# A new order of all steps, and of the products of zeros between them, in a fused local-attention and feed-forward kernel

## The chip, the core and the metric

The kernel runs on one core of a Trainium2 chip. A core has a matrix engine (TensorE, PE in the rows; its loads of stationary operands are PEld), a vector engine (DVE), a scalar engine with function tables (ACT), a general engine (GpSimd, POOL) and an engine that here issues all transfers (SyncE, SP). Each runs its own list of instructions in order; an instruction that needs another engine's result waits on a semaphore, and all that stands behind it on its engine waits too. The metric is the device time of one execution in microseconds.

## What is computed

```python
scores = scale * np.matmul(q, k.transpose(0, 1, 3, 2))        # q, k, v: 8 x 8 heads x 576 x 64
mask_plain = (rel >= 0) & (rel < 32)                          # heads 0 to 3
mask_dil = (rel >= 0) & (rel < 128) & (rel % 4 == 0)          # heads 4 to 7
scores = np.where(masks, scores, -1e9); scores -= max
attn = np.exp(scores); attn = attn / (sum + 1e-9)
x = (attn @ v) -> 4608 tokens x 512
h = x @ w_in                                                  # 512 x 2048
sp = np.where(h > 20.0, h, np.log1p(np.exp(np.minimum(h, 20.0))))
out = (h * np.tanh(sp)) @ w_out                               # mish, then 2048 x 512
```

The weights arrive as 64-bit floats. Products run in 16-bit floats with each operand split into a high and a low part, three products for one.

## The kernel before

The work is cut into sixteen units (a batch and half of its 576 rows each, 288 tokens). For one unit the steps are: loads of q and k (`ld`) and of v (`lv`), scales and splits of these (`pr`), scores of a pair of heads on PE (`sp`), the row maximum on DVE (`sc`), exponentials on ACT (`ex`), a transpose of the probabilities (`tp`: on PE for the first four units, by a transposing DMA for the others), the product with v and the division (`va`: PE, ACT, DVE), the transpose of the result (`tx`), then the feed-forward part: scales (`fs`), sixteen first products with mish on ACT (`ff`), the split of a quarter of the hidden layer (`gt`: ACT and DVE, for five quarters ACT and GpSimd), and sixteen second products of twelve matmuls (`fo`), the last of each four followed by scaling and a store.

The weights are prepared beside the first units, in pieces: load (`wl`), a pass of ACT over the upper words (`wm`), the rebuilding of 32-bit words on DVE (`ww`, lines 397 to 401), a sum over partitions on PE with a scale from it on DVE (`ws`, lines 367 to 388), and the split into high and low halves (`wp`, lines 412 to 426: ACT and DVE, for some pieces also GpSimd). `w.0.3.1` style numbers mean layer, column block, half.

Nothing plans at run time: a table of names, `ORDER`, fixes the order of all steps of all engines. A step is a generator; each time its name comes up it issues its next part, so that `va1.4` stands three times: products, denominators, division. The instructions of each engine run in the order in which they are issued:

```python
for name in ORDER:
    if name not in begun:
        ...
        if name[:2] == "kw":
            fn(int(name[2:]))
            continue
        begun[name] = fn(...)
    if hasattr(begun[name], "__next__"):
        next(begun[name], None)
```

`kwN` issues N products of a 128 x 128 block of zeros (line 922) into the last of four PSUM banks that `ff` and `fo` take in turn. They compute nothing that is used; they fill time in which PE's next real work isn't ready. `fs` (lines 831 to 833) makes small scales on DVE. Lines 759 and 761 are the reciprocal and the division of `va`, lines 717, 787 and 790 transposes on PE, line 804 the lower half of a transposed result.

Of the kernel before, what the change touches and what calls it, by code (L numbers as in the profile page):

```python
# [42 lines left out]
va0.1 sp0.1 tp0.7 va0.1 kw2 va0.7 ld1 sc0.2 wp0.0.1 sc0.3 va0.7 va0.1 ex0.2 pr1 kw16 kw16 kw7 tp0.4 ex0.3 kw5 tp0.2
kw13 tx0.0 wm0.1.0 va0.7 wp0.0.0 kw10 tx0.3 tp0.4 tp0.2 ww0.1.0 tx0.0 wl0.2.1 kw16 kw1 va0.2 tx0.3 ww0.1.0 tx0.0 tx0.0
kw11 tx0.3 va0.4 va0.2 va0.4 kw2 tp0.5 tx0.3 va0.2 tp0.5 va0.4 kw16 tp0.3 va0.5 wp0.0.1 sp1.0 va0.5 tp0.3 va0.5
wm0.2.0 wl0.1.1 sc1.0 kw8 sp1.1 sc1.1 ex1.0 sc1.2 kw14 va0.3 wm0.2.1 tx0.2 lv2 sc1.3 kw2 pr1 va0.3 tx0.2 va0.3 ex1.3
pr1 kw16 kw6 tx0.2 ww0.2.0 tp1.0 ld2 tx0.2 tx0.1 pr1 ww0.2.1 tx0.1 fs0.0 ex1.2 pr1 kw16 kw1 tx0.1 ws0.2 tx0.1 tp1.0
ww0.2.1 ff0.12 ex1.1 wm0.1.1 ff0.13 ff0.12 ww0.1.1 ws0.2 va1.0 tp1.2 ff0.13 tp1.1 ff0.14 ww0.2.0 va1.0 wp0.2.1 ws0.1
ff0.14 tp1.1 ff0.15 va1.0 tp1.2 wp0.2.0 ws0.1 va1.2 ww0.1.1 ff0.15 ff0.0 va1.2 wp0.1.0 sp1.2 ff0.0 gt0.3 tp1.3 sc1.4
ff0.3 wp0.1.1 va1.2 ff0.2 sc1.5 tp1.3 ff0.3 wp0.2.0 sp1.3 ff0.2 ex1.4 wp0.2.1 va1.1 wl1.3.0 va1.3 ff0.1 sc1.7 va1.1  # L50
va1.3 ex1.5 sc1.6 ff0.8 ex1.7 va1.3 va1.1 ex1.6 tp1.4 ff0.9 fs0.2 ff0.1 wp0.1.1 tx1.0 tx1.1 wp0.1.0 ff0.8 ff0.11 tx1.0
tp1.4 gt0.3 wl1.3.1 gt0.0 tp1.5 tx1.0 va1.4 wl1.1.0 ff0.10 fs1 tp1.5 gt0.0 tx1.1 wl1.1.1 ff0.9 tx1.1 ff0.4 tx1.0 pr2
wm1.3.0 va1.5 va1.4 tp1.6 ff0.11 tp1.7 tp1.6 fs0.1 ff0.7 va1.5 va1.4 ff0.10 tp1.7 va1.5 ff0.4 va1.6 va1.7 va1.6
wm1.3.1 tx1.2 va1.6 lv3 ff0.6 va1.7 tx1.2 va1.7 gt0.2 ww1.3.1 kw7 tx1.3 tx1.2 sp2.0 ww1.3.0 tx1.3 gt0.0 ff0.5 sc2.1
tx1.2 ff0.7 tx1.3 ws1.3 ff0.6 gt0.2 tx1.3 ff0.5 sc2.0 ff1.8 ex2.1 ws1.3 pr2 ff1.4 pr2 ex2.0 ww1.3.0 ff1.5 wm1.1.0
tp2.0 ff1.8 sp2.1 ww1.1.0 ww1.1.0 pr2 ff1.11 ld3 ff1.4 wm1.1.1 ff1.10 tp2.0 ww1.1.1 ff1.5 pr2 ff1.9 ff1.11 gt0.1 sc2.2
ff1.6 sc2.3 wp1.3.0 gt0.1 ws1.1 ff1.10 wp1.3.0 ff1.9 ex2.2 ff1.0 ww1.3.1 wl1.2.1 ff1.7 ex2.3 ws1.1 va2.0 ff1.6 tp2.2
tp2.1 fo0.3.0 ww1.1.1 tp2.2 va2.0 va2.2 wp1.3.1 ff1.2 ff1.0 wp1.3.1 fo0.3.1 tp2.1 wp1.1.0 wp1.1.1 wl1.2.0 fo0.3.2
va2.0 wp1.1.1 pr3 fo0.3.3 va2.2 wm1.2.1 va2.1 wp1.1.0 ff1.7 sp2.3 va2.2 fo0.3.3 ff1.3 wp1.1.1 sc2.6 ww1.2.1 wl1.0.0
va2.1 gt1.2 fo0.1.0 sc2.7 wp1.1.1 va2.1 wm1.2.0 fo0.1.1 gt1.2 wl1.0.1 ff1.2 sp3.2 ff1.3 fo0.3.3 ww1.2.0 ex2.7 gt1.2  # L60
ff1.1 sc3.4 ex2.6 fo0.1.2 ww1.2.1 gt1.1 sp3.1 ex3.4 fo0.1.3 sc3.2 gt1.1 ff1.1 ff1.12 sc3.5 gt1.1 sc3.3 tp2.3 ff1.12
ws1.2 tp2.3 ww1.2.0 gt1.0 va2.3 ws1.2 wm1.0.0 ff1.13 va2.3 sp3.0 va2.3 fo0.1.3 tp2.7 sc3.0 tx2.0 tp2.7 ff1.14 wm1.0.1
gt1.0 tx2.0 ff1.15 wp1.2.1 tx2.0 sc3.1 tp2.6 fo1.1.0 ff1.13 ww1.0.0 ff1.15 ww1.0.1 ex3.0 sp2.2 ws1.0 sc2.4 ld4 ex3.1
sc2.5 ex2.4 wp1.2.1 fo1.3.0 tp2.6 ex2.5 wp1.2.0 tx2.1 fo1.1.1 ww1.0.0 ff1.14 ws1.0 wp1.2.0 va2.6 fo1.3.1 tx2.1 va2.6
wp1.0.0 va2.7 wp1.2.0 tx2.1 tp2.4 fo1.3.2 va2.6 tx2.1 wp1.2.0 va2.7 tp2.4 va2.7 fo1.1.2 gt1.3 pr4 ex3.5 tx2.3 gt1.3
pr3 va2.4 fo1.2.0 gt1.3 tx2.3 fo1.2.1 va2.4 tx2.3 wp1.0.0 pr3 tp2.5 pr3 tp3.0 tp2.5 pr3 fo1.1.3 tp3.0 va2.4 wp1.0.0
ww1.0.1 va2.5 fo0.2.0 ex3.2 wp1.0.0 tp3.1 fo1.3.3 tp3.1 va2.5 va2.5 va3.0 pr4 tx2.2 fo1.2.2 tx2.2 fo1.1.3 fo1.1.3
# [911 lines left out]
```

## Time and profile before

| | us |
|---|---|
| median of 3 runs (lowest to highest) | 930.99 (930.51 to 931.06) |
| profiled execution | 931.03 |
| its span | 929.2 |
| PE busy | 918.5 (99%) |
| DVE busy | 647.5 (70%) |
| ACT busy | 565.7 (61%) |
| GpSimd busy | 57.3 (6%) |
| products of zeros, busy | 42.0, 646 of them |

A busy share is an average over the whole span: it counts products of zeros like others, and in the first 60 us PE's busy time is mostly these. Matmuls overlap in the pipeline, so a row's time for some matmuls in a row is longer by the tail of the last than the distance to the next row's start. Rows in order of time give the start, the duration, the engine, the line, the instruction with its tiles, how many, and in brackets how long the engine sat idle before and for whom. Waits are listed by who waited for whom.

### The profile page before, as it was taken

Reading aid. Unit: us, or ns where it says so; the run is one execution under the profiler, and the core shown is the slowest. Engines: PE = TensorE matmul, PEld = TensorE weight load, DVE = VectorE, ACT = ScalarE, POOL = GpSimd, SP = SyncE. Lnnn points to the kernel's source line nnn. Section 1 sums busy time; section 2 is a strip of 40 time slices with the busy share of each in tenths; the row PEclk is TensorE's granted clock in tenths of the full one; section 3 lists DMA queues with packets and bytes.
Section 4 is the critical chain, followed back from the end, with each engine's and each line's share of the span. In section 5 each row is a group of like instructions: output and inputs, shape, how many; then the busy total and the mean of one; then the engine's idle time right before and its main releaser. Section 6 shows DMA issues by size and latency. Waiting matters only on the chain.

```text
span 929.2 us, 22966 instructions
## 1 busy us (share of the span) xinstructions
PE 918.5 (99%) x9558; PEld 745.0 (80%) x9562; DVE 647.5 (70%) x1352; ACT 565.7 (61%) x1086; POOL 57.3 (6%) x116
## 2 busy tenths in 40 slices
PE   9999999999999989999999999999999999999998
PEld 9988877888778778788878888877888787888876
DVE  4998987558585697997687887877686786524120
ACT  2888977566666547577566665747576563745241
POOL 1001064401000000000000000000000000000000
PEclk9999999999999999999999999999999999999999
DMA  7656341121413225262517232535315322121100
GB/s 258 196 167 209 114 143 52 59 74 42 96 40 98 76 70 131 58 146 43 141 29 155 60 112 45 119 89 93 89 40 100 79 55 61 28 68 41 47 1 26
DMA packets 158104, 82.44 MB, mean 89 GB/s; under 512 B 124496, under 2 KB 153904, under 8 KB 158000
## 3 DMA queue, kind: packets, MB, share of 16 engines
q1 hardware_dynamic: 158000, 80.97, 35.0%
q8 instruction: 75, 1.23, 0.5%
q14 instruction: 29, 0.24, 0.1%
...
## 4 chain that ended last, share of the span: by engine, by line
PE 92%; DVE 5%; ACT 1%; issue 1%; DMA 0%; SPq 0%; DVEq 0%; ACTq 0%
PE f L894 39%; PE f L843 38%; PE psc L617 4%; PE f L922 3%; PE pav L744 3%; PE pav L738 1%; PE ptp L717 1%; DVE raw L399 1%; DVE nm L648 1%; DVE m L309 1%; DVE raw L401 0%; PE psc L614 0%; ACT hm L848 0%; DVE raw L412 0%; PE pm L367 0%
## 5 line engine op out<-in xcount | busy, mean ns | idle before, releaser
L843 PE MATMUL f<-x,w 128*128 128x288 f16 x3072 | 393.3, 286 | 1.7 <-ACT hm L848 1.7
L894 PE MATMUL f<-g,w 128*128 128x288 f16 x3072 | 393.2, 287 | 0.0
L894 PEld LDWEIGHTS <-w 128*128 128x128 f16 x3072 | 296.7, 98 | 74.9
L843 PEld LDWEIGHTS <-w 128*128 128x128 f16 x3072 | 295.5, 98 | 76.0 <-issue 2.2
L848 ACT ACTIVATE hm<-f,fs 128x288 f32<-128x288 f32 x256 | 119.6, 497 | 103.5 <-PE f L843 96.8
L884 DVE SCALAR_TENSOR_TENSOR g<-hm,sg,g 128x1152 f16<-128x1152 f32 x59 | 82.9, 1409 | 40.5 <-ACT g L882 40.5
L906 ACT ACTIVATE y<-f,fo 128x288 f32<-128x288 f32 x60 | 41.8, 718 | 99.6 <-PE f L894 74.2
L882 ACT ACTIVATE g<-hm,sg 128x1152 f16<-128x1152 f32 x59 | 73.9, 1253 | 0.6
L759 DVE RECIPROCAL rec<-den 96x3 f32<-96x3 f32 (+1 forms) x128 | 21.3, 167 | 68.1 <-ACT den L755 56.5
L650 DVE TENSOR_TENSOR sb<-sb,nm 96x256 f32<-96x256 f32 (+3 forms) x120 | 56.4, 470 | 4.1
L761 DVE TENSOR_TENSOR xs<-pav,rec 96x192 f32<-96x192 f32 (+1 forms) x128 | 49.6, 387 | 11.2 <-DVE rec L759 0.9
L648 DVE TENSOR_REDUCE nm<-sb 96x2 f32<-96x256 f32 (+3 forms) x120 | 53.7, 448 | 3.3
L670 ACT ACTIVATE sb<-sb,ln_p 96x352 f32<-96x352 f32 (+3 forms) x96 | 53.5, 586 | 0.2
L755 ACT ACTIVATE den<-pav 96x3 f32<-96x3 f32 (+1 forms) x96 | 14.7, 162 | 62.8 <-PE pav L744 62.5
...
L642 DVE SCALAR_TENSOR_TENSOR sb<-psc,sc,m_r 96x352 f32<-96x352 f32 (+1 forms) x48 | 28.4, 592 | 24.3 <-PE psc L617 24.1
L922 PE MATMUL f<-zeros 128*128 128x128 f16 x646 | 42.0, 224 | 1.1 <-DVE zeros L918 1.1
...
L922 PEld LDWEIGHTS <-zeros 128*128 128x128 f16 x646 | 39.1, 101 | 1.9 <-DVE zeros L918 1.0
L776 ACT CAST g<-xs 96x384 f16<-96x384 f32 (+1 forms) x48 | 26.8, 562 | 19.9 <-DVE xs L761 17.6
L642 DVE SCALAR_TENSOR_TENSOR sb<-psc,sc,m_s 72x288 f32<-72x288 f32 (+1 forms) x48 | 27.6, 574 | 11.3 <-PE psc L617 11.2
...
## 6 DMA issues: line engine op xcount, KB each, us to landing
...
```

Source lines behind the costliest of these rows:

```text
L642: nc.vector.scalar_tensor_tensor(shaped(sb), shaped(pt), d["sc"][:nq], mask, ALU.mult, ALU.add)
L648: nc.vector.tensor_reduce(nm[:nq, j:j + n], x, axis=AX.X, op=ALU.max, negate=True)
L650: nc.vector.tensor_tensor(o, x, nm[:nq, j:j + n].unsqueeze(2).broadcast_to([nq, n, w]), op=ALU.add)
L670: nc.scalar.activation(x, x, AF.Exp, bias=ln_p[:nq])
L761: nc.vector.tensor_tensor(xs[:nq, :nb, (head % 2) * D:(head % 2 + 1) * D], avv[:, :, :D], rc.unsqueeze(2).broadcast_to([nq, nb, D]), op=AL ...
L843: nc.tensor.matmul(ph[:, :HT], w1[j][:, c, wi, k * P:(k + 1) * P], x_of(d, xi, c), start=(n == 0), stop=(n == len(seq) - 1))
L848: nc.scalar.activation(d["m"][j][:, k], ph[:, :HT], AF.Mish, scale=d["fs"][:, j:j + 1])
L882: nc.scalar.activation(g[:, 0], m, AF.Identity, scale=sg)
L884: nc.vector.scalar_tensor_tensor(g[:, 1], m, sg, g[:, 0], ALU.mult, ALU.subtract)
L894: nc.tensor.matmul(po[:, :HT], w2[:, e, j, wi, k * P:(k + 1) * P], d["g"][j][:, gi, k, :], start=(j == 0 and n == 0), stop=(j == NCH - 1 a ...
L906: nc.scalar.activation(o, src, AF.Identity, scale=fo)
L922: nc.tensor.matmul(fbs[3][:, 512 - P:], zeros, zeros, start=True, stop=True)
```

## The change

Only the table `ORDER` is another one. Each step stands in it as often as before; the `kw` entries alone differ in number: 54 entries with 646 products before, 52 with 598 now. Before, 639 of the products stand before the first `ff` step and 7 behind the fifteenth; now 553 stand before the first, and 28, 2, 6 and 9 behind the eighth, ninth, eleventh and twelfth. The table's first line, before and after:

```diff
 ORDER = """
-lv0 wl0.3.0 wl0.3.1 ld0 wl0.0.0 wl0.0.1 pr0 kw16 kw16 kw16 kw16 kw16 kw16 kw16 kw16 kw3 pr0 pr0 kw10 pr0 wm0.3.0
+wl0.3.1 wl0.3.0 ld0 lv0 wl0.0.1 wl0.0.0 wm0.3.1 ww0.3.1 ww0.3.1 wm0.3.0 ww0.3.0 ww0.3.0 kw16 kw16 kw16 kw16 kw16 kw16
```

What it moves is seen in the engines' lists. The transfer queue SP at its start, before: values of unit 0 (`vn`, `vdn`), then the first two pieces of weights (`raw`), then q and k.

```order
L473 DMA vn<-in_v 128x4x64 x3
L475 DMA vdn<-in_vd 72x4x64 x4
L341 DMA raw<-in_w_in 128x512 x4
L447 DMA qn<-in_qT 128x1152
L449 DMA knp<-in_kT 128x2x288
L452 DMA knd<-in_kdT 128x4x72 x2
L341 DMA raw<-in_w_in 128x512 x6
```

SP at its start now:

```order
L341 DMA raw<-in_w_in 128x512 x4
L447 DMA qn<-in_qT 128x1152
L449 DMA knp<-in_kT 128x2x288
L452 DMA knd<-in_kdT 128x4x72 x2
L473 DMA vn<-in_v 128x4x64 x3
L475 DMA vdn<-in_vd 72x4x64 x4
L341 DMA raw<-in_w_in 128x512 x8
```

The four weight transfers moved from behind the seven of the values to the head, and the values behind q and k. DVE follows: the two reductions over unit 0's values (line 309) stood first there, and stand now behind the first weights' split (line 418).

The second place is DVE near the end of unit 2's attention. Before, `ws` is the scale chain of a piece of the second layer (its last two rows here), line 412 two passes over raw weights, lines 759 and 761 the two divisions that fill `xs`, which PE transposes next; line 804 is the lower half of that transpose.

```order
L387 RECIPROCAL r_o_2599<-f_o_105 128x1
L388 TENSOR_SCALAR ws4_2593<-f_1_104,r_o_2599 128x4
L412 TENSOR_SCALAR raw_2207<-raw_2207,ws4_2593 128x512 x2
L759 RECIPROCAL rec_2651<-den_2622 72x4
L761 TENSOR_TENSOR xs_2608<-pav_2603,rec_2651 72x4x64
L759 RECIPROCAL rec_2659<-den_2656 72x4
L761 TENSOR_TENSOR xs_2608<-pav_2626,rec_2659 72x4x64
L309 TENSOR_REDUCE m_2677<-qn_2536 128x1
L804 TENSOR_TENSOR x_2440<-px_2681,x_2440 128x4x72
```

The same two divisions and what follows them now:

```order
L759 RECIPROCAL rec_2561<-den_2555 72x4
L761 TENSOR_TENSOR xs_2525<-pav_2520,rec_2561 72x4x64
L397 TENSOR_SCALAR w2_103<-w2_103 128x1024
L759 RECIPROCAL rec_2586<-den_2582 72x4
L761 TENSOR_TENSOR xs_2525<-pav_2564,rec_2586 72x4x64
L399 SCALAR_TENSOR_TENSOR raw_2177<-raw_2177,w2_103 128x1024
L397 TENSOR_SCALAR w2_103<-w2_103 128x1024
L399 SCALAR_TENSOR_TENSOR raw_2340<-raw_2340,w2_103 128x1024
L804 TENSOR_TENSOR x_2445<-px_2611,x_2445 128x4x72
L418 SCALAR_TENSOR_TENSOR w2_103<-raw_1948,ws4_2310,w2_103 128x512 x2
L374 TENSOR_REDUCE wm4_2671<-pm_2627 128x4
```

The scale chain (it begins with line 374) and the raw passes moved behind the transpose's lower half, and work on weight words (lines 397, 399) stands among the divisions.

The third place is DVE and PE in unit 1's attention, where unit 0's first `ff` products are under way. DVE now:

```order
L418 SCALAR_TENSOR_TENSOR w_100<-raw,ws_1435,w_100 128x2x512
L831 TENSOR_SCALAR fs<-f_104,f 128x1
L832 RECIPROCAL sg<-fs 128x1
L833 TENSOR_SCALAR sg<-sg 128x1
L759 RECIPROCAL rec<-den 72x4
L761 TENSOR_TENSOR xs<-pav,rec 72x4x64
```

In the old list one scale step of unit 1, on four columns at once, stood near this place, behind a gate; now two steps of unit 0 do, on one column each, ahead of and behind a division. PE now, down to the first of nine zeros, behind which the next transpose (`ptp`) waits for the division above:

```order
L843 MATMUL f_111<-x,w_101 128x288
L717 MATMUL ptp<-ident,sb 104x72 x4
L790 MATMUL px<-ident,xs 128x96 x3
L738 MATMUL pav<-vdn,pp 72x65 x4
L922 LDWEIGHTS zeros
L922 MATMUL f_111<-zeros 128x128
```

PE before, at the same transposes of unit 1, with no zeros among them:

```order
L843 MATMUL f_108<-x,w_100 128x288
L738 MATMUL pav<-vdn,pp 72x65 x4
L717 MATMUL ptp<-ident,sb 104x72 x8
L843 LDWEIGHTS w_100
L843 MATMUL f_109<-x,w_100 128x288
```

The last two transposes of the unit's probabilities stood together between `ff` products; now one stands ahead of the nine zeros and one behind.

## Rows read from the trace of the kernel before

**Rows 1.** The page's first part: busy time, share and instructions of each engine.

```profile
PE 918.5 (99%) x9558; PEld 745.0 (80%) x9562; DVE 647.5 (70%) x1352; ACT 565.7 (61%) x1086; POOL 57.3 (6%) x116
```

**Rows 2.** PE's waits: line, for whom; us in total, times, longest.

```profile
PE px L790 <- DVE xs L761: 1.9, 1, 1.9
PE f L843 <- ACT hm L848: 1.7, 2, 1.2
PE pav L744 <- DMA pT<-p: 1.6, 1, 1.6
PE f L922 <- DVE zeros L918: 1.1, 1, 1.1
PE px L787 <- ACT pp L726: 0.3, 1, 0.3
PE ptp L717 <- DVE rec L759: 0.2, 1, 0.2
```

**Rows 3.** PE in order of time: start, the first ff products, the end.

```profile
1.05 9.35 PE L922 MATMUL f<-zeros 128*128 128x128 f16 x131 [1.05 <-DVE zeros L918]
...
11.30 7.71 PE L922 MATMUL f<-zeros 128*128 128x128 f16 x135
18.85 1.06 PE L367 MATMUL pm<-w,ones 128*128 128x512 bf16 x3
...
58.34 3.10 PE L843 MATMUL f<-x,w 128*128 128x288 f16 x24
...
901.83 23.68 PE L894 MATMUL f<-g,w 128*128 128x288 f16 x192
```

**Rows 4.** Stretches: length, busy PE, PEld, DVE, ACT, POOL, granted clock, DMA, GB/s.

```profile
21.50:55.10 33.60, 33.09 (x510) 30.08 (x509) 31.07 (x73) 25.57 (x66) 0.24 (x2) 1.00 0.68 210
155.00:165.00 10.00, 8.13 (x61) 5.99 (x59) 4.97 (x15) 3.98 (x7) 5.99 (x5) 0.83 0.01 2
340.00:900.00 560.00, 560.00 (x5762) 449.56 (x5761) 385.63 (x799) 334.57 (x642) 8.18 (x53) 1.00 0.35 76
```

**Rows 5.** The transfer queue SP in order of time, at the start.

```profile
6.31 2.02 SPq L341 DMA_DIRECT2D raw<-in_w_in  x4
```

**Rows 6.** ACT in order of time, the first passes over weights.

```profile
13.53 1.16 ACT L356 ACTIVATE w<-raw 128x1024 f32<-128x1024 f32 x1 [2.70 <-DMA raw<-in_w_in]
16.06 1.17 ACT L356 ACTIVATE w<-raw 128x1024 f32<-128x1024 f32 x1 [1.37 <-DMA raw<-in_w_in]
```

**Rows 7.** DVE in order of time, at the start.

```profile
5.42 0.95 DVE L309 TENSOR_REDUCE m<-vn 128x1 f32<-128x768 f32 x1 [4.42 <-DMA vn<-in_v]
8.13 1.22 DVE L309 TENSOR_REDUCE m<-vdn 72x1 f32<-72x1024 f32 x1 [1.76 <-DMA vdn<-in_vd]
...
22.64 0.16 DVE L379 RECIPROCAL ws<-f 128x1 f32<-128x1 f32 x1
```

**Rows 8.** PE in order of time, around its longest wait.

```profile
152.51 3.11 PE L894 MATMUL f<-g,w 128*128 128x288 f16 x24
157.49 0.44 PE L790 MATMUL px<-ident,xs 72*128 72x72 f32 x4 [1.87 <-DVE xs L761]
...
158.40 4.78 PE L894 MATMUL f<-g,w 128*128 128x288 f16 x24
```

**Rows 9.** DVE in order of time, ahead of that wait.

```profile
150.72 1.15 DVE L375 TENSOR_SCALAR wf<-wm 128x4 int32<-128x4 int32 x1
...
152.96 2.81 DVE L412 TENSOR_SCALAR raw<-raw,ws 128x512 int32<-128x512 int32 x2
```

**Rows 10.** GpSimd in order of time, the same stretch.

```profile
149.03 2.81 POOL L422 TENSOR_TENSOR raw<-raw 128x1024 f32<-128x1024 f32 x1 [14.42 <-DVE raw L412]
153.07 2.36 POOL L426 TENSOR_TENSOR w<-raw,w 128x1024 f16<-128x1024 f32 x1 [1.23 <-ACT w L424]
```

**Rows 11.** DVE in order of time, a small scale in unit 1's attention.

```profile
82.10 1.14 DVE L833 TENSOR_SCALAR sg<-sg 128x4 f32<-128x4 f32 x1
```

**Rows 12.** GpSimd in order of time, the second half of a gate.

```profile
89.28 2.38 POOL L879 TENSOR_TENSOR g<-hm,g 128x1152 f16<-128x1152 f32 x1
```

More of the change, by code (lines that the diff above doesn't have):

```diff
@@ L43 @@
[L43 to L67, printed above, removed]
@@ new lines @@
+tx1.3 sc2.0 ff0.6 gt0.2 ff0.7 ff1.8 gt0.1 ww1.3.1 ff1.10 ex2.0 ff1.0 fs1 ex2.1 ws1.3 tp2.0 ff1.2 tp2.0 gt0.1 ff1.8
+sp2.1 ww1.3.0 sp2.3 wm1.1.1 ld3 ff1.4 ff1.10 ff1.0 sc2.2 ff1.2 ff1.9 wp1.3.0 ww1.1.1 ff1.11 wm1.1.0 wp1.3.0 ff1.6
+ff1.9 ww1.1.0 ff1.4 wl1.2.1 ff1.11 sc2.3 ff1.1 ff1.6 ww1.1.0 ex2.2 fo0.3.0 ff1.3 sc2.7 wp1.3.1 sc2.6 ws1.1 fs2 ex2.3
+wp1.3.1 ex2.6 ff1.5 ws1.1 wl1.2.0 gt1.2 sp3.2 wp1.1.0 gt1.2 fo0.3.1 sc3.4 gt1.2 fo0.3.2 ex3.4 fo0.3.3 ww1.1.1 ff1.1
+sc3.5 wp1.1.0 tp2.1 sp3.1 fo0.3.3 ff1.3 va2.0 fo0.3.3 ff1.12 ff1.5 wp1.1.1 wl1.0.0 gt1.0 sc3.2 lv3 ff1.15 wp1.1.1
@@ new lines @@
+va2.0 tp2.1 sc3.3 wm1.2.0 ff1.7 gt1.0 wm1.2.1 va2.1 tp2.2 ww1.2.1 ff1.13 tp2.2 ww1.2.0 wp1.1.1 ww1.2.0 ws1.2 ff1.12
+ff1.15 ww1.2.1 va2.1 ff1.7 fo0.1.0 ex2.7 fo0.1.1 ws1.2 wp1.1.1 gt1.1 ff1.14 va2.0 gt1.1 va2.1 wl1.0.1 tp2.3 va2.2
+wp1.2.0 tp2.3 sp3.0 ff1.13 gt1.1 fo0.1.2 sc3.1 va2.2 ff1.14 sc3.0 va2.3 ex3.1 fo1.3.0 wp1.2.0 va2.2 pr3 tp2.6 ex3.5
+fo0.1.3 va2.3 tp2.6 gt1.3 va2.3 tx2.0 tp2.7 fo1.3.1 tp2.7 gt1.3 tx2.0 wm1.0.0 tx2.0 sp2.2 gt1.3 fo0.1.3 wm1.0.1
+fo1.1.0 sc2.4 fo0.1.3 sc2.5 ld4 ex3.0 wp1.2.0 va2.6 fo1.3.2 ex2.5 wp1.2.0 fo1.1.1 va2.6 ex2.4 va2.6 va2.7 ww1.0.0
@@ new lines @@
+gt5.2 tx6.1 pr8 tx6.1 ff5.15 ff5.13 pr8 va6.6 fo5.0.0 gt5.2 va6.4 va6.5 pr8 sp7.0 va6.5 ff5.14 fo5.0.1 va6.4 ff5.15
+gt5.3 sc7.0 pr8 fo5.0.2 tx6.3 fo5.1.0 pr8 gt5.3 fo5.1.1 va6.5 fo5.1.2 va6.4 sc7.1 tx6.2 sp7.3 pr8 fo5.0.3 sc7.6
+fo5.1.3 sc7.7 pr8 fo5.2.0 fo5.1.3 fo5.2.1 pr8 ex7.0 fo5.1.3 fo5.2.2 ex7.2 pr8 fo5.2.3 fo5.0.3 tp7.2 ex7.1 tp7.2
+fo5.3.0 ex7.5 tx6.3 pr8 tx6.2 tx6.3 sp8.1 fo5.3.1 tx6.2 ex7.3 fo5.3.2 tp7.5 fo5.0.3 ex7.4 tp7.5 tp7.2 tp7.4 pr8
+fo5.3.3 tp7.3 ld9 tp7.0 ex7.7 ff6.0 fo5.3.3 tp7.3 tp7.4 fo5.2.3 sp8.3 tp7.0 tp7.1 ff6.1 sc8.2 ff6.0 tp7.0 ff6.2 tp7.5
@@ new lines @@
+ff6.1 sc8.7 ff6.3 tp7.4 ff6.2 sc8.3 ex7.6 ff6.4 ff6.3 pr9 lv9 va7.0 ff6.5 pr9 tp7.7 ff6.6 ff6.4 tp7.1 va7.0 sc8.6
+tp7.1 ff6.7 ff6.6 gt6.0 pr9 tp7.3 sp8.0 va7.0 ff6.5 ff6.8 ff6.7 gt6.0 ff6.9 ff6.8 pr9 gt6.1 va7.2 ff6.10 tp7.6 va7.2
+sc8.0 pr9 va7.1 ff6.11 va7.1 ff6.9 ff6.10 va7.2 pr9 va7.3 ff6.11 ff6.12 va7.3 gt6.2 va7.1 gt6.1 ff6.13 pr9 va7.3
+ff6.14 sc8.1 ff6.15 ff6.12 gt6.2 tx7.0 ff6.14 fo6.0.0 ff6.15 tx7.0 ff6.13 tp7.6 tx7.0 pr9 sp8.2 tp7.7 fo6.0.1 sc8.5
+tp7.7 va7.4 sc8.4 tp7.6 fo6.0.2 va7.4 tx7.1 gt6.3 fo5.3.3 pr9 fo6.1.0 fo5.2.3 ex8.3 va7.5 fo6.1.1 tx7.1 ex8.4 gt6.3
@@ new lines @@
+ex14.0 gt12.3 tp13.7 fo12.1.1 va13.4 tp14.0 pr15 ex14.1 va13.2 fo12.1.2 va13.2 tp14.1 va13.3 fo12.0.3 va13.3 va13.2
+tp14.0 tp14.1 fo12.1.3 va13.3 va13.5 fo12.2.0 pr15 tx13.2 ex14.7 ex14.5 fo12.2.1 fo12.0.3 tx13.2 tx13.2 va13.6
+fo12.2.2 va13.6 ex14.4 tp14.0 tx13.1 fo12.1.3 fo12.2.3 tx13.1 va13.6 fo12.1.3 tp14.1 va13.7 fo12.3.0 va13.7 ex14.6
+va13.7 fo12.0.3 tp14.5 fs13 tx13.1 tx13.3 fo12.3.1 pr15 tx13.3 sp15.1 tx13.3 fo12.3.2 ex14.3 pr15 fo12.2.3 fo12.3.3
+tp14.6 sp15.3 sc15.2 fo12.3.3 ff13.0 tp14.3 tp14.4 tp14.4 ff13.1 ff13.0 tp14.6 sc15.3 ff13.2 ff13.1 tp14.7 tp14.5
@@ new lines @@
+tx15.1 fo14.2.3 tx15.1 tx15.1 fo14.3.0 tx15.2 fo14.3.1 fo14.1.3 fo14.3.2 fo14.3.3 ff15.0 fo14.3.3 fo14.2.3 fo14.3.3
+ff15.1 ff15.0 fo14.2.3 ff15.2 ff15.3 ff15.2 ff15.1 ff15.4 ff15.3 gt15.0 ff15.5 ff15.4 gt15.0 ff15.6 ff15.7 ff15.8
+ff15.7 ff15.5 ff15.6 ff15.9 ff15.8 ff15.10 ff15.11 ff15.10 gt15.1 ff15.12 ff15.9 ff15.11 ff15.13 gt15.2 ff15.12
+ff15.14 gt15.2 ff15.13 gt15.1 ff15.15 fo15.0.0 ff15.15 ff15.14 gt15.3 fo15.0.1 gt15.3 fo15.0.2 fo15.1.0 fo15.1.1
+fo15.1.2 fo15.0.3 fo15.1.3 fo15.2.0 fo15.1.3 fo15.1.3 fo15.2.1 fo15.2.2 fo15.2.3 fo15.3.0 fo15.2.3 fo15.0.3 fo15.2.3
@@ L191 @@
+fo15.3.1 fo15.0.3 fo15.3.2 fo15.3.3 fo15.3.3 fo15.3.3
 """.split()
```

248 lines of the change are left out of this document (121 added, 127 removed).

## Prediction

> **What bounds the kernel now.** The first line of the page comes first: TensorE (PE) is busy for 918.5 of 929.2 us, and DVE, the next, for 70% [rows 1]. So the question is not how fast the other engines are, but whether PE ever waits for them. The list of PE's waits answers it: 1.1 us at the very start, until the zeros are written, and then 5.7 us in six waits, of which three are over 1 us [rows 2]. After PE's last product begins its tail, 901.83 + 23.68 = 925.5 us, only the last scaling and store follow, 3.7 us [rows 3]; the last steps of the new list are the same ones.
>
> PE at 99% does not mean that all its work is needed. 646 of its products are of zeros (`kw` steps), and all but 7 stand before the first product of the feed-forward part, which starts at 58.34 us [rows 3]. In those first 58 us PE is waiting for the other engines in another dress. There DVE is the engine that sets the pace: from the first weight scale on it is busy for 31.07 of 33.6 us [rows 4], and what is missing is small gaps between dependent instructions. It goes on as densely until the first layer's weights are split; after that PE has its fill of real work.
>
> **What a change of the order alone can move.** Every step of the old list is in the new one, as often as before; only the zeros differ. So the end moves by three things: the zeros that PE runs, the time it waits, and the time it runs at the lower clock. I sum these against the profiled execution, 931.03 us, of which 929.2 is the span and 1.83 lies around it; the median of the three runs shown is 930.99, so the difference doesn't matter.
>
> *The zeros.* The old list has 646, the new one 598, so 48 go. 135 of them in a row took from 11.30 to 18.85 us, 55.9 ns each [rows 3]: 48 x 0.0559 = 2.68 us. They run on PE, which sets the end, and they fill gaps that the list foresees, so their number says how much waiting each list expects. This is a gain only if the waits that they stood for are really gone. In place: 86 fewer before the first ff product (553 for 639), and 45 new ones among the first ff products of unit 0 for 7.
>
> *Is the wait at the start really shorter?* In the old order the queue SP sends unit 0's values first and the first weights at 6.31 us [rows 5]; ACT's first pass over weights starts at 13.53 and the second at 16.06, when each pair has landed [rows 6]. In the new order both weight pairs are at the head of the queue. The first pair can't land before the time at which the three small value loads, then at the head, reached DVE (5.42 us), and hardly after the time when all seven had (8.13) [rows 7]; the second came 2.53 us behind the first [rows 6], which makes 8 to 10.7 us. ACT and DVE need about 2 us more to prepare the sums, 10 to 12.7 us. PE gets to the first sum over weights after 234 zeros: 1.05 us, 131 in 9.2 us and 103 x 0.0559 = 5.8 us, so at 16.0 us, not 18.85 [rows 3], and does not wait for it. The scale, which DVE finished at 22.80 (its last step 22.64 + 0.16) [rows 7], is then ready near 16.0 + 1.1 + 1.3 = 18.4 us, 4.4 earlier. Against that, the preparation of unit 0's values (0.95 + 1.22 us and some 1.2 us of small steps) lay before the weights, where DVE had nothing else [rows 7], and now lies in DVE's dense stretch: net gain there about 1 us.
>
> *Does DVE reach the first ff product in time?* PE could be there at 58.34 - 86 x 0.0559 - 1.6 (other products that moved behind it) = 51.9 us. DVE needed 33.5 us from 21.55 to the end of unit 0's last needed value. In the new order 7.6 us of that (one weight split 1.27, one word build 2.45, four heads of scores 3.9) come later and 3.9 us (the value preparation and one small scale) come into it, so 29.8 us; with the start at 17.1 and a wait of 1.5 us for the first scores that is 48.4, and the last transpose, its lower half and two groups of scores take PE about 4 us: 52.4. So the two are level within my error of 1 us: there is no reserve at the start, and each microsecond that DVE is late there is one at the end. I take the list at its word here and put the term at 2.68 us; between its ends it can be worth nothing.
>
> *The long wait.* At 155.6 us PE waits 1.87 us for DVE [rows 8]. The releaser is the division of unit 2's values, and on DVE the two instructions ahead of it are stretched: a step on 128 x 4 numbers took 1.15 us, where a small step of the start took 0.16 [rows 7], and two passes over raw weights took 2.81 us [rows 9]. Both times GpSimd runs a long instruction beside them, 149.03 to 151.84 and 153.07 to 155.43 [rows 10], and the small DVE step ends at 151.87, 0.03 us behind GpSimd's. So DVE was held until GpSimd was done; that cost it about 1.0 + 1.9 us. In the new order the scale chain and the raw passes stand behind unit 2's last transpose, and the two divisions that PE waits for follow one conversion of weights (L397), with score steps before; that wait should go: 1.87 us.
>
> *The clock.* Right behind that wait the granted clock is 0.83 over 10 us [rows 4]: PE falls from 2.4 to 1.2 GHz for a while. The 24 products from 158.40 took 4.78 us where 24 like them took 3.11 [rows 8]: 1.67 us, gone with the wait.
>
> *The other waits.* 1.7 us for mish, 1.6 us for a transposing DMA, 0.5 us in all for small ones [rows 2]. Transposes through the DMA queue stand in the new list at much the same distance from the products that use them, the mish steps too, and nothing in the change speaks against waits of that size somewhere. I let these 3.8 us stand: their ends are 0 and a few times as much.
>
> **Sum.** 931.03 - 2.68 - 1.87 - 1.67 = 924.8 us.
>
> **The rivals.** *No new waits at all:* the 3.8 us go too, 921.0. For it speaks that from 340 to 900 us PE was busy throughout [rows 4]; against it, that three of the old waits came unforeseen, and a new order brings new ones.
>
> *GpSimd holds DVE at another place.* In the new order the gate of unit 0's first column block runs on GpSimd while DVE has ahead of it the small scales (L831 to L833, twice) and the division that PE's next transpose needs; only 9 zeros, 0.5 us, stand before that. In the old order such a scale took 1.14 us beside the first half of that gate [rows 11]; the second half takes 2.38 us [rows 12]. That is up to 2.38 - 0.5 = 1.9 us of wait over the reserve and, if it is like the old one, 1.67 us of slow clock: 924.8 + 3.6 = 928.4. Against it speaks that DVE is held only where one of its instructions starts while GpSimd's is running, and the list may well leave it 2 us here that I can't see. The Trainium skill has a rule on this ("SBUF — State Buffer", Who interferes with whom): DVE and GpSimd share one pair of ports, which an instruction holds until it ends, so that the second to ask is blocked, not slowed, and DVE's steps with one scalar are among those that ask. The trace agrees where the small step ends 0.03 us behind GpSimd's [rows 9, 10]. By the rule alone both small scales would be held here and the time would be this rival's 928.4; by the same meeting in the old order [rows 11], after which PE waited for nothing [rows 2], it stays at 924.8.
>
> *Nothing gained:* DVE is late by the 2.7 us that the zeros save and the long wait comes back elsewhere: 931.0.
>
> *Slower, by the clock:* in the stretch that DVE paces, 16 to 82 us, fewer zeros stand between PE's short pieces, in gaps of the list's own reckoning. If DVE is late there PE runs dry, and a wait like the old one costs 1.87 + 1.67 = 3.54 us. Past 932.85 it takes 8.05 us, so from the third such wait on; three give 935.4. For it: no reserve at the start. Against it: in the old list the waits there were 0.5 us in all with DVE as full.
>
> That the engines run another order than the list can be left out: the rows of the new order show the moves.
>
> **How the numbers follow.** 0.40 for 924.8 (alone some 923 to 927), 0.12 for 921.0, 0.20 for 928.4, 0.13 for 931.0, 0.15 for slower. A measurement of this kernel can tell about 0.2%, 1.9 us, from no change. So faster 0.72, same 0.13, slower 0.15. The range runs from just under the case without waits, 920.5, to 932.5: it leaves out most of the slower case and a little below.
>
> **What would show it.** Right: 598 zeros at 56 ns; the first sum over weights near 16 us without a wait, the first ff product near 52; no wait at unit 2's last transpose and a granted clock of 1.0 around 150 us; PE's waits after the first microsecond under 5 us. Wrong: a row among PE's waits of 2 us or more with a clock below 1.0 behind it; or a first ff product after 55 us, which means that DVE, not the list, sets the start.

## The result

The changed kernel takes 933.49 us at the median (928.98 to 936.01 over 20 runs), the kernel before, run beside it, 930.96 (929.96 to 931.48). The ratio is 1.0025, with an interval of 1.0014 to 1.0035: slower by a quarter of a percent, where 924.8 was forecast and 932.5 was the end of the range. The profiled execution took 935.6 us with a span of 933.5. It is the second longest of the twenty, so what its rows cost is set against 935.6, not against the median.

First the page's busy line and PE's waits in the changed kernel (line, for whom; us in total, times, longest), against [rows 1, 2]:

```profile
PE 920.9 (99%) x9514; PEld 745.0 (80%) x9514; DVE 651.1 (70%) x1352; ACT 568.1 (61%) x1088; POOL 57.1 (6%) x116
```

```profile
PE pm L327 <- DVE dg L324: 3.6, 1, 3.6
PE psc L614 <- DVE xs L761: 3.2, 1, 3.2
PE f L922 <- DVE zeros L918: 1.1, 1, 1.1
PE f L843 <- DMA x<-g: 0.4, 1, 0.4
```

All old waits over 1 us are gone: the division (1.9), mish (1.7), the transposing DMA (1.6). Two new ones stand in their place, 3.6 and 3.2 us, both for DVE. PE has 44 instructions fewer than before and is nevertheless busy for 2.4 us longer. The rows in order of time show why. PE at the start, and around the two waits, against [rows 3, 8]:

```profile
1.05 15.21 PE L922 MATMUL f<-zeros 128*128 128x128 f16 x234 [1.05 <-DVE zeros L918]
16.10 1.06 PE L367 MATMUL pm<-w,ones 128*128 128x512 bf16 x4
...
51.86 4.58 PE L843 MATMUL f<-x,w 128*128 128x288 f16 x36
...
132.87 1.63 PE L843 MATMUL f<-x,w 128*128 128x288 f16 x12
...
138.43 1.02 PE L614 MATMUL psc<-m_fb,ident_b 96*96 96x384 bf16 x2 [3.20 <-DVE xs L761]
...
140.92 3.06 PE L894 MATMUL f<-g,w 128*128 128x288 f16 x12
...
189.85 0.58 PE L327 MATMUL pm<-dg,ones 5*128 5x5 f32 x2 [3.58 <-DVE dg L324]
...
191.81 3.08 PE L843 MATMUL f<-x,w 128*128 128x288 f16 x12
```

Twelve products took 1.63 us ahead of the first wait and 3.06 and 3.08 behind the two: half speed. The stretches show how much of it there is (length, busy PE, PEld, DVE, ACT, POOL, granted clock, DMA, GB/s; against [rows 4]):

```profile
135.00:150.00 15.00, 11.80 (x82) 8.64 (x82) 10.03 (x24) 7.97 (x15) 5.57 (x4) 0.77 0.09 33
150.00:165.00 15.00, 14.98 (x160) 12.61 (x158) 10.88 (x25) 8.97 (x22) 4.26 (x3) 1.00 0.32 90
186.00:206.00 20.00, 16.42 (x121) 13.03 (x120) 11.77 (x23) 9.59 (x17) 3.77 (x10) 0.83 0.31 94
```

At two levels, 1.2 and 2.4 GHz, a mean of 0.77 over 15 us is 2 x 0.23 x 15 = 6.9 us at the lower one, and 0.83 over 20 us is 6.8. Half of that is lost: 3.4 us behind each wait. Around 157 us, where the old long wait was, the clock is 1.00.

What held DVE stands beside it on GpSimd (POOL). DVE first, then GpSimd, in the same two places:

```profile
133.77 1.05 DVE L375 TENSOR_SCALAR wf<-wm 128x4 int32<-128x4 int32 x1
...
135.06 2.21 DVE L384 TENSOR_TENSOR wf<-wf,f 128x4 f32<-128x4 f32 x1
...
185.34 4.45 DVE L324 TENSOR_SCALAR dg<-ident,c 5x5 f32<-5x5 f32 x1
```

```profile
133.65 1.15 POOL L877 TENSOR_SCALAR g<-hm 128x1152 f16<-128x1152 f32 x1 [1.60 <-ACT hm L874]
134.88 2.36 POOL L879 TENSOR_TENSOR g<-hm,g 128x1152 f16<-128x1152 f32 x1
...
184.92 0.94 POOL L687 MEMSET p<- 96x1024 f16 x1
...
188.82 0.66 POOL L688 MEMSET pT<- 128x688 f16 x1
...
189.61 0.16 POOL L499 MEMSET m<- 128x5 f32 x1
```

The step of 133.77 ends at 134.82, GpSimd's of 133.65 at 134.80; the step of 135.06 ends at 137.27, GpSimd's at 137.24. Where nothing of GpSimd's runs beside them both take under 0.2 us (g5, below). In the second place a product of 5 x 5 numbers begins at 185.34 and ends at 189.79. It sat out the six memsets of `open_late`, which follow each other without a gap (the first and the last are shown), and five small ones behind them, the last of which ends at 189.77. In the kernel before the same product came at 187.38, 0.1 us behind the six, and took 0.22 us. (The five small ones ran beside it there and did not lengthen it.) So the old order missed this meeting by 0.1 us, and the new one walked into it. PE's waits follow: the first division that the scores need comes behind the scales on DVE and ends at 138.4.

The trace has more holds of this kind. Line 388 took 0.81 us at 115.13 and line 653 took 1.77 us at 116.64, and PE waited for neither. Line 401 took 3.04 us at 130.10, where 1.23 is usual; it makes DVE late for the chain of scales, but it stands in g5 too (below), where PE waits only 0.28 us.

**The theory to test:** the loss is these two holds of DVE by GpSimd (3.2 and 3.6 us of wait) and the lower clock behind each (1.7 to 3.4 us). **The rivals:** DVE is late in these places because of the order itself, and the holds are only what it happened to be doing; or the clock falls for a reason other than the waits.

### The profile page after: what moved, and what is told of

The parts are those of the page before. It is cut to its first block, busy times and chain, and to the rows that moved or that the text cites. A ratio compares the mean times of both kernels' runs of the same rounds, so it can differ in the third digit from the quotient of the medians.

```text
span 933.5 us, 22894 instructions
## 1 busy us (share of the span) xinstructions
PE 920.9 (99%) x9514; PEld 745.0 (80%) x9514; DVE 651.1 (70%) x1352; ACT 568.1 (61%) x1088; POOL 57.1 (6%) x116
## 4 chain that ended last, share of the span: by engine, by line
PE 92%; DVE 6%; ACT 1%; issue 1%; DMA 0%; DVEq 0%; SPq 0%; ACTq 0%
PE f L894 39%; PE f L843 38%; PE psc L617 4%; PE pav L744 3%; PE f L922 3%; PE pav L738 1%; DVE raw L401 1%; PE ptp L717 1%; DVE raw L399 1%; DVE w L418 1%; PE psc L614 0%; DVE dg L324 0%; DMA x<-g 0%; DVE nm L648 0%; DVE xs L761 0%
## 5 line engine op out<-in xcount | busy, mean ns | idle before, releaser
L759 DVE RECIPROCAL rec<-den 72x4 f32<-72x4 f32 (+1 forms) x128 | 21.3, 167 | 59.5 <-ACT den L755 45.4
L650 DVE TENSOR_TENSOR sb<-sb,nm 96x256 f32<-96x256 f32 (+4 forms) x120 | 55.7, 464 | 4.1
L761 DVE TENSOR_TENSOR xs<-pav,rec 72x256 f32<-72x256 f32 (+1 forms) x128 | 49.6, 387 | 10.3
L648 DVE TENSOR_REDUCE nm<-sb 96x2 f32<-96x256 f32 (+4 forms) x120 | 53.7, 448 | 3.3
L670 ACT ACTIVATE sb<-sb,ln_p 72x288 f32<-72x288 f32 (+3 forms) x96 | 53.4, 586 | 1.6 <-DVE sb L650 1.4
L922 PE MATMUL f<-zeros 128*128 128x128 f16 x598 | 39.5, 225 | 1.1 <-DVE zeros L918 1.1
L922 PEld LDWEIGHTS <-zeros 128*128 128x128 f16 x598 | 36.9, 102 | 1.8 <-DVE zeros L918 1.0
L708 DVE TENSOR_TENSOR g<-sb,g 72x288 f16<-72x288 f32 (+3 forms) x39 | 20.2, 520 | 22.8 <-ACT g L706 22.8
```

The source lines that it names most:

```text
L648: nc.vector.tensor_reduce(nm[:nq, j:j + n], x, axis=AX.X, op=ALU.max, negate=True)
L650: nc.vector.tensor_tensor(o, x, nm[:nq, j:j + n].unsqueeze(2).broadcast_to([nq, n, w]), op=ALU.add)
L670: nc.scalar.activation(x, x, AF.Exp, bias=ln_p[:nq])
L708: nc.vector.tensor_tensor(lo, src, hi, op=ALU.subtract)
L761: nc.vector.tensor_tensor(xs[:nq, :nb, (head % 2) * D:(head % 2 + 1) * D], avv[:, :, :D], rc.unsqueeze(2).broadcast_to([nq, nb, D]), op=AL ...
L922: nc.tensor.matmul(fbs[3][:, 512 - P:], zeros, zeros, start=True, stop=True)
```

## Experiments

Each run is the changed kernel with the edit shown, unless another kernel is named. All ran beside the kernel before on the same chip, which gave 930.3 to 931.0 us.

**Two edits that missed their place (e1, e4), and what they are good for.** Both aimed at unit 4's 5 x 5 product, but the condition `u == FIRST` names unit 3, whose preparation has no such product. So both are the changed kernel once more. e1 was meant to make the product on ScalarE (ACT), e4 to fill PE's wait with zeros:

```
+            if on_act:
+                nc.scalar.activation(dg[:n, :n], ident[:n, :n], AF.Identity, scale=c[:n])
...
+            mr = yield from over_partitions(m, 5, u == FIRST)
```

> The changed kernel with one edit: in unit 4's prep the 5x5 product dg of L324 is made by ScalarE (idle from 185.5 to 191.2 us in the changed kernel's profile) instead of VectorE. Theory (GpSimd's six memsets of 184.9 to 189.5 us hold VectorE's 5x5 product for 4.45 us where it took 0.22 in the kernel before; TensorE waits 3.58 us for it and then runs 6.83 us at the half clock, which costs 3.41): the wait on dg falls from 3.6 to under 0.5 us and the half-clock stretch at 190 us goes: 933.5 - 3.6 - 3.4 = 926.5 us, between 925.5 and 930 as the other fall comes or not. Rival A (VectorE is simply late there, or whoever makes dg is held as long): the wait stays, 933.5. Rival B (the clock falls for another cause than the wait): only 3.6 is gained, 929.9, and a half-clock stretch stays near 190 us.

> The changed kernel with one edit: 60 products of zeros (60 x 0.0559 = 3.35 us) stand in TensorE's queue ahead of the product that waits for dg in unit 4's prep, so that the 3.58 us are filled with work that nobody needs. Nothing else is changed, the wait on VectorE's dg stays as long. Theory (the half-clock stretch behind it comes from TensorE having stood still): it goes, and with it 3.4 us, while the wait's own 3.6 us stay: 933.5 - 3.4 = 930.1 us, between 928.9 and 932.5. Rival (the clock falls for another cause, or the slow stretch is worth nothing): 933.5, half-clock stretch at 190 us as before.

Measured: 933.86 and 934.47 us, ratios of 1.004 (1.0028 to 1.0052) and 1.0029 (1.0016 to 1.0043), with the waits of 3.6 and 3.2 us in both. They repeat the result and show how much varies from one execution to the next: in e1's profile the granted clock was 0.89 at 135 to 150 us, in e4's 0.77, that is 3.3 and 6.9 us at the lower level behind waits of the same length.

**The divisions ahead of the scales (e2, e3).** The two divisions that PE waits for are put on DVE ahead of the scales of ws1.2, which GpSimd holds. One line of the list changes:

```
-... fo0.1.1 ws1.2 wp1.1.1 gt1.1 ff1.14 va2.0 gt1.1 va2.1 wl1.0.1 ...
+... fo0.1.1 va2.0 va2.1 ws1.2 wp1.1.1 gt1.1 ff1.14 gt1.1 wl1.0.1 ...
```

> The changed kernel with one edit: the divisions of unit 2's heads 0 and 1 stand ahead of the second step of ws1.2 on VectorE, not behind it. Theory (unit 3's scores wait 3.20 us because that chain of scales is held by GpSimd's gate, 1.05 and 2.21 us where 0.17 and 0.16 are usual, and the divisions queue behind it): with the divisions done by about 134.2 us the wait of 3.2 goes, and with it the half-clock stretch at 138 to 145 us, 3.4: 933.5 - 6.6 = 926.9 us, between 925.8 and 930.5. The hold itself stays, on the chain of scales, with nobody waiting for it. Rival A (the chain was what TensorE needed soon after anyway): a wait of 2 to 3 us comes up on the weights of ws1.2 a few us later, 931 to 933.5. Rival B (the clock falls for another cause): 930.3.

Measured: 929.64 us (928.16 to 931.03), ratio 0.9989 (0.998 to 0.9997); 3.9 us less than the changed kernel, or 3.4 if each is taken against the kernel before beside it. That is inside the stated range, but well short of the 6.6 us of the theory; why is said at f3. e3 is this and the misplaced edit of e1, so it is the same program again:

> The changed kernel with both edits of the first two runs. Theory: both waits (3.58 and 3.20 us) and both half-clock stretches (3.41 each) go: profiled 935.6 - 13.6 = 922.0 us, and a median of 922 to 923 with a narrow spread, under the 931.0 of the kernel before, granted clock 0.998. Rival (the lost time turns into new waits of the same size behind those two places): 926 to 930. Rival B (half-clock stretches are not tied to the waits): 926.7 and a spread as wide as now.

Measured: 929.74 us (925.11 to 930.87), ratio 0.9985 (0.9975 to 0.9995). PE's wait at the scores and the clock behind it in e2, and then DVE there:

```profile
PE psc L614 <- DVE xs L761: 0.4, 1, 0.4
```

```profile
135.00:150.00 15.00, 14.27 (x143) 11.40 (x142) 12.99 (x30) 12.91 (x27) 10.46 (x7) 1.00 0.31 99
```

```profile
134.54 0.35 DVE L761 TENSOR_TENSOR xs<-pav,rec 96x192 f32<-96x192 f32 x1
...
135.74 2.23 DVE L382 TENSOR_SCALAR wf<-wf 128x4 f32<-128x4 f32 x1
```

GpSimd holds the chain of scales as before (its gate's second half runs from 135.57 to 137.94, and L382 ends at 137.97), but nobody waits for that chain now. The wait of 3.2 us is 0.4, and the clock is 1.00. The first rival, that the chain is needed at once anyway, falls: no wait of 2 to 3 us came up behind. The time alone, near the second rival's 930.3, wouldn't decide on the clock; the 1.00 does.

**The chain left where it is, GpSimd's work taken away (g5).** That alone doesn't tell a hold from an order. So in g5 the chain stays ahead of the divisions, and the gate beside it leaves GpSimd; DVE does its second half behind the divisions. (Here and in f1, f3, f7 unit 4's 5 x 5 product is on ACT, see the next run.)

```
-ON_POOL = {(0, 0), (1, 1), (1, 2), (1, 3), (2, 1)}
+ON_POOL = {(0, 0), (1, 2), (1, 3), (2, 1)}
...
-... ws1.2 wp1.1.1 gt1.1 ff1.14 va2.0 gt1.1 va2.1 wl1.0.1 ...
+... ws1.2 wp1.1.1 gt1.1 ff1.14 va2.0 va2.1 gt1.1 wl1.0.1 ...
```

> The run f1 (dg on ScalarE: 928.9 us, with the wait of 3.2 us at unit 3's scores left) with GpSimd's gate of unit 1's second chunk taken off GpSimd: VectorE makes the low half in one step of about 1.4 us, and that step stands behind the two divisions. The scales of ws1.2 stay ahead of the divisions, as in the changed kernel. Theory (the wait came from GpSimd holding two small steps of that chain, 1.05 and 2.21 us in place of 0.17 and 0.16): without GpSimd's work beside them both take under 0.2 us, the first division ends near 135.3 us and the wait falls from 3.2 to about 0.4 us, with no half-clock stretch behind it: 928.9 - 2.8 - 1.7 to 3.4 = 922.7 to 924.4 us. Rival A (the order alone, the chain standing ahead of the divisions, makes the wait): 3 us stay, 928.9. Rival B (VectorE's 1.4 us more come out behind): 925 to 927 with a new wait of 1 to 2 us.

Measured: 923.57 us (922.28 to 924.16), ratio 0.9919 (0.9905 to 0.9932). DVE, and then PE at the scores:

```profile
133.07 0.17 DVE L378 TENSOR_SCALAR wf<-wm 128x4 int32<-128x4 int32 x1
133.28 0.17 DVE L385 TENSOR_SCALAR wf<-wf 128x4 f32<-128x4 f32 x1
133.48 0.16 DVE L387 TENSOR_TENSOR wf<-wf,f 128x4 f32<-128x4 f32 x1
...
135.15 1.40 DVE L887 SCALAR_TENSOR_TENSOR g<-hm,sg,g 128x1152 f16<-128x1152 f32 x1
```

```profile
134.81 0.83 PE L617 MATMUL psc<-m_fb,ident_b 96*96 96x384 bf16 x2 [0.28 <-DVE xs L764]
```

The same steps in the same order take 0.17 and 0.16 us where they took 1.05 and 2.21, and PE waits 0.28 us. The two steps are 2.93 us shorter together, and the wait is 2.92 us shorter. So the order alone doesn't make the wait; GpSimd's hold does. DVE pays 1.40 us for the gate that it now does itself, and the time is none the worse for it.

**Unit 4's 5 x 5 product on ACT (f1).** The edit of e1 in the right place:

```
+            mr = yield from over_partitions(m, 5, u == FIRST + 1)
```

> The changed kernel with one edit: the 5x5 product dg (L324) of unit 4's prep, the one that took 4.45 us, is made by ScalarE; unit 5's stays on VectorE. (In the run e1 the condition named unit 3, whose prep has no such product, so that run was the changed kernel once more: 933.9 us, with the wait of 3.6 us.) Theory (the six memsets of GpSimd hold VectorE's product; ScalarE, idle from 185.5 us on, isn't held): dg ready by about 185.8 us in place of 189.8, the wait of TensorE on it falls from 3.6 to under 0.5 us, the half-clock stretch behind it goes: 933.5 - 3.6 - 3.4 or 1.7 = 926.5 to 928.2 us. Rival A (whoever makes it is held as long): 933.5, wait of 3.6. Rival B (clock falls for another cause): 929.9 with a half-clock stretch near 190 us.

Measured: 928.85 us (927.82 to 929.67), ratio 0.9981 (0.9972 to 0.999). In four views ACT's product, PE's use of it, what DVE did meanwhile, and the stretch:

```profile
184.99 0.28 ACT L325 ACTIVATE dg<-ident,c 5x5 f32<-5x5 f32 x1
```

```profile
185.73 0.38 PE L330 MATMUL pm<-dg,ones 5*128 5x5 f32 x2
```

```profile
186.41 2.92 DVE L303 TENSOR_SCALAR f<-m 128x3 int32<-128x3 int32 x1
```

```profile
184.00:204.00 20.00, 20.00 (x188) 16.43 (x187) 14.32 (x32) 13.63 (x26) 5.31 (x12) 1.00 0.38 112
```

ACT took 0.28 us for it beside the first of the memsets, PE doesn't wait, and the clock stays at 1.00. The time is 0.65 us over the forecast range (see f3). The hold itself is still there: it now falls on DVE's next small step (2.92 us), which PE doesn't need.

**Is it the standing still that costs the clock (f4)?** PE is given 60 products of zeros ahead of the product that waits, DVE's work is as in the changed kernel.

```
+        for _ in range(fill):
+            nc.tensor.matmul(pm[:, 384:512], zeros, zeros, start=True, stop=True)
...
+            mr = yield from over_partitions(m, 5, 60 if u == FIRST + 1 else 0)
```

> The changed kernel with one edit: 60 products of zeros (60 x 0.0559 = 3.35 us) in TensorE's queue ahead of the product that waits for unit 4's dg; the wait on VectorE's dg (held by GpSimd as before) is as long, but TensorE works through it. (In the run e4 the condition named unit 3 and put in none: the changed kernel once more, 934.5 us.) Theory (the half-clock stretch comes from TensorE having stood still for 3.6 us): the granted clock of 184 to 204 us is 1.0 in place of 0.83 to 0.91, the product of dg still begins near 189.8 us, and 1.7 to 3.4 us are gained: 930.1 to 931.8. Rival (the clock falls there for another cause): 933.5 and 0.83 to 0.91 as before.

Measured: 931.34 us (930.66 to 933.6), ratio 1.0013 (1.0004 to 1.0022), 2.2 under the changed kernel, or 1.5 if each is taken against the kernel before beside it. PE, DVE's product, and the stretch:

```profile
185.53 3.51 PE L327 MATMUL pm<-zeros 128*128 128x128 f16 x60
188.97 0.38 PE L329 MATMUL pm<-dg,ones 5*128 5x5 f32 x2
```

```profile
184.77 2.04 DVE L324 TENSOR_SCALAR dg<-ident,c 5x5 f32<-5x5 f32 x1
```

```profile
184.00:204.00 20.00, 20.00 (x218) 17.07 (x217) 11.88 (x26) 10.33 (x19) 5.22 (x12) 1.00 0.31 94
```

From the start of the 24 products ahead of it (182.84; 183.16 in the changed kernel) PE came to its real product 6.13 us later, against 6.69, having worked on zeros instead of standing still, and the clock is 1.00 in place of 0.83. From that product to the end of the span it takes 740.2 us, against 743.6 in the changed kernel: about the 3.4 us that the lower clock had cost there. So the fall of the clock is a cost of the standstill. The medians give less, since the profiled execution of the changed kernel had more of the lower clock than over half of its twenty. One thing wasn't as expected: DVE's product was held for 2.04 us this time, until the third memset's end; it got in between two of them. So the length of this hold varies from execution to execution.

**Both causes taken away (f3, twice).**

> The changed kernel with the divisions ahead of the scales of ws1.2 (as in e2) and unit 4's dg on ScalarE. e2 gave 929.6 us (and the same program again 929.7) with no half-clock stretch at 135 to 150 us and the wait on dg of 3.6 left. Theory: that wait and its half-clock stretch (3.41 or 6.83 us long, so 1.7 or 3.4 lost) go: 929.7 - 3.6 - 1.7 to 3.4 = 922.7 to 924.4 us, granted clock 1.0, spread under 1 us. Rival (a new wait of that size appears behind): 926 to 930.

> The run f3 once more (divisions ahead of the scales, dg on ScalarE), beside the other two on the same chip: 923.8 us again, between 923.2 and 924.5, no half-clock stretch between the start and the last 5 us. Rival (its narrow spread was luck, the clock falls in part of the executions): some executions at 925 to 928.

Measured: 923.84 us (923.20 to 924.39), ratio 0.9931 (0.9918 to 0.9943), and 923.96 (923.72 to 924.94), ratio 0.9926 (0.9914 to 0.9938). The longest of PE's waits that are left, and the two stretches:

```profile
PE f L925 <- DVE zeros L921: 1.0, 1, 1.0
PE f L846 <- DMA x<-g: 0.5, 1, 0.5
```

```profile
135.00:150.00 15.00, 14.28 (x140) 11.27 (x139) 12.49 (x28) 12.45 (x25) 9.60 (x6) 1.00 0.30 96
...
184.00:204.00 20.00, 20.00 (x201) 16.47 (x199) 15.12 (x36) 13.52 (x25) 0.00 (x0) 1.00 0.44 130
```

With both holds out of PE's way the new order is worth 9.0 to 9.6 us more than as it was, each taken against the kernel before beside it, and the spread shrinks from 7 us in twenty executions to 1.2 in each run of five. One edit alone gave less than its forecast, because the forecasts took what was read from the profiled execution (935.6 us) off the median (933.5). Between the profiled executions the first edit gave 5.2 us (e2), the second 6.6 (f1) and both 12.1 (f3): there the two add up.

**What are the zeros at the start worth (f7)?** f3 with 24 products of zeros fewer ahead of the first sum:

```
-... kw16 kw16 kw16 kw10 ws0.3 ws0.3 kw16 kw15 ...
+... kw16 kw16 kw2 ws0.3 ws0.3 kw16 kw15 ...
```

> The run f3 (both waits taken away, 923.8 us) with 24 products of zeros fewer ahead of the first sum of TensorE (210 for 234 at the start). In the changed kernel's profile the words that the sum needs are ready at 14.4 us and TensorE comes to it at 16.1. Theory (the zeros at the start are on the path, 56 ns each): the sum at 14.8 us, the first feed-forward product 1.34 us sooner, 923.8 - 1.3 = 922.5 us. Rival (VectorE, busy with the next words until 16.9 us, takes the sum's maximum only then, 0.27 us sooner than now, and sets the rest): 923.5.

Measured: 922.2 us (922.05 to 922.41), ratio 0.9906 (0.9891 to 0.9921), the best of all here, 1.8 under the run of f3 beside it, of which 1.3 were expected. PE:

```profile
1.04 13.59 PE L925 MATMUL f<-zeros 128*128 128x128 f16 x210 [1.04 <-DVE zeros L921]
14.80 1.06 PE L370 MATMUL pm<-w,ones 128*128 128x512 bf16 x4 [0.16 <-DVE w L400]
...
50.58 3.60 PE L846 MATMUL f<-x,w 128*128 128x288 f16 x28
```

The first sum comes 1.30 us sooner than in the changed kernel, and the first ff product 1.28; against the second run of f3, beside it, both come 1.2 us sooner (16.03 and 51.78 there). The rest of the 1.8 us fits the waits for x<-g, 0.6 us in that run's trace, of which f7's has none. DVE doesn't take it back: it has slack for that much between the first scale and the first scores. PE now waits 0.16 us for the words, so there is no more to be had in this place.

**The old wait taken out of the old order (e8).** The kernel before, with unit 2's divisions of heads 6 and 7 ahead of the held scales of ws1.0:

```
-... ff1.14 ws1.0 wp1.2.0 va2.6 ... va2.6 wp1.0.0 va2.7 ... va2.7 fo1.1.2 ...
+... ff1.14 wp1.2.0 va2.6 ... va2.6 va2.7 ... va2.7 ws1.0 wp1.0.0 fo1.1.2 ...
```

> The kernel before with one edit: unit 2's divisions of heads 6 and 7 stand ahead of the second step of ws1.0 and the first of wp1.0.0 on VectorE, which the profile before shows held by GpSimd (1.15 and two of 2.81 us). This takes the old long wait alone out of the old order, without the other changes. Theory (the wait of 1.87 us at 157 us and the half-clock stretch behind it, 1.67, hang on that): 930.5 - 3.5 = 927.0 us on this chip where its clock fell to 0.83, 928.6 in executions in which it didn't fall; the granted clock there 1.0. Rival (the scales are needed soon after, and a wait of 1 to 2 us comes up on the weights of ws1.0): 929 to 931.

Measured: 931.62 us (928.95 to 932.0), ratio 1.0011 (1.0003 to 1.002); no gain. PE, then DVE:

```profile
155.76 0.42 PE L790 MATMUL px<-ident,xs 72*128 72x72 f32 x4
...
162.13 0.38 PE L327 MATMUL pm<-c,ones 1*128 1x1 f32 x2 [2.13 <-DVE c L321]
```

```profile
155.60 1.08 DVE L382 TENSOR_SCALAR wf<-wf 128x4 f32<-128x4 f32 x1
...
157.30 1.84 DVE L388 TENSOR_SCALAR ws<-f,r_o 128x4 f32<-128x4 f32 x1
```

The wait at 157 us [rows 8] is gone, as expected, and one of 2.13 us has come up 5 us later, for DVE again: the chain was held all the same (1.08 and 1.84 us), and now the maxima of a next unit's q queue behind it. The clock didn't stay at 1.00 either, as the theory had it, but fell behind the new wait:

```profile
150.00:165.00 15.00, 12.87 (x114) 10.44 (x113) 11.15 (x25) 9.02 (x17) 10.09 (x7) 0.92 0.09 22
165.00:184.00 19.00, 19.00 (x173) 15.55 (x172) 9.40 (x25) 8.11 (x18) 6.77 (x4) 0.97 0.21 68
```

The rival was nearest: it had about the right size (1 to 2 us, 929 to 931) and named another place. Taking one wait away by reordering was worth nothing here, as the hold fell ahead of something else that PE needs.

## Why the prediction was wrong, step by step

**The zeros: right.** 598 of them, 234 at the start until 16.10 us (forecast 16.0), the scale ready at 18.46 (18.4), the first ff product at 51.86 (51.9). Products of zeros keep PE busy for 39.5 us in place of 42.0, which is 2.5 us for the 2.68 of the sum. That they are on the path is shown for 24 of them by f7, and that also shows that DVE had a reserve of 1.3 us at the start, where the prediction saw none. To meet the start within 0.1 us was partly luck, for it varies: behind the same 234 zeros the first sum began at 15.38 us in g5's trace and at 16.85 in f4's. The weights came later than estimated: the words were ready at 14.4 us, not by 12.7, still 1.7 us before PE.

**The long wait and its clock: right where they were, wrong as a gain.** No wait at unit 2's last transpose, clock 1.00 from 150 to 165 us. But the same new order put another scale chain, that of ws1.2, beside a gate on GpSimd, and unit 4's 5 x 5 product among the memsets, both ahead of a step that PE needs. e8 shows that taking away the old wait alone gains nothing: 931.62 us.

**"I let these 3.8 us stand": this is the step that failed.** The mish and DMA waits under that name went, and two holds came: the waits after the first microsecond are 7.6 us in all, not 3.8. The price of a new wait was missing from the sum altogether, since the old small waits had no slow clock behind them and the new ones have 3.4 us each. On the profiled execution: 924.8 + 3.8 + 2 x 3.4 = 935.4, against 935.6 measured.

**The rival "GpSimd holds DVE at another place": right in kind, wrong in place, number and size.** It was priced once, at 928.4, at the gate of unit 0 around 82 us. There PE waited 0.18 us. The small steps there write one number a row, and the changed kernel's rows show that such a step isn't held; GpSimd's second half of the gate runs beside it from 80.55 to 83.76:

```profile
81.89 0.15 DVE L833 TENSOR_SCALAR sg<-sg 128x1 f32<-128x1 f32 x1
```

The row it was priced by [rows 11] has 128 x 4 numbers. The rule of the Trainium skill that the prediction set beside it ("SBUF — State Buffer", Who interferes with whom: the second to ask for the shared ports is blocked until the first is done) is borne out by the ends in the two places above, 0.02 to 0.03 us behind GpSimd's. What I didn't read from the rows is that GpSimd's instructions in an unbroken row can hold one DVE step through all of them (4.45 us). Which steps are held could in part have been told beforehand: a page of the Trainium skill ("VectorE: DVE Perf Modes", What auto-detection actually checks) says that a step enters a two-port mode if its one source and its destination lie in SBUF and their outermost dimensions longer than one are both even or equal. The trace agrees: steps with one source on 5 x 5, 128 x 3 and 128 x 4 numbers were held (4.45, 2.92 and 1.05 us), and those on 128 x 1, which have no such dimension, were not (0.15). The sentence doesn't cover line 384, which has two sources and was held for 2.21 us.

**The price of a wait: too low.** 1.87 + 1.67 was taken from one row. The two new ones cost 3.20 + 3.4 and 3.58 + 3.4 in the profiled execution. In the rival "slower, by the clock" three waits were needed to pass 932.85; two of this size were enough, and they came at 138 and 190 us, behind the stretch of 16 to 82 us where I looked for them.

**What the sum was worth.** f3 is the new order without the two holds in PE's way: 923.8 to 924.0 us. The forecast of 924.8 would have been near for the order, though with some luck: f3's waits behind the first microsecond are 1.6 us and not the 3.8 that the sum let stand, so the same sum with these would give 922.6. The loss of 9.0 to 9.6 us lies in GpSimd's hold on a few DVE steps that need 0.2 us each.

**What stays open.** The executions of the changed kernel range from 929.0 to 936.0, the clock over the whole span from 0.998 to 0.992. Three things that vary are shown: how much lower clock follows a wait (3.3 to 6.9 us), how long the memsets hold DVE (2.04 to 4.46 us), and when the first sum begins (15.38 to 16.85 us). Two of the last, the zeros ahead of that sum in g5 and in f4:

```profile
1.04 14.49 PE L925 MATMUL f<-zeros 128*128 128x128 f16 x234 [1.04 <-DVE zeros L921]
...
1.04 15.97 PE L924 MATMUL f<-zeros 128*128 128x128 f16 x234 [1.04 <-DVE zeros L920]
```

That the quickest executions are those with a short hold and little lower clock fits, and so does the one of 925.1 us of e3, but only one execution of each kernel has a trace, so it isn't shown. Nor was it tried to move the memsets themselves.

The kernel before varies as well: of its 64 executions beside the experiments 30 had a mean clock of 1.000 (930.0 to 930.2 us on average by chip) and 34 one of 0.998 (931.0 to 931.3), so the 1.67 us that the forecast took for its clock was there to be gained in about half of them, if that fall is the one behind its long wait.
